# Strassen's seven products for K, three Q blocks and two feature groups, placed ahead of attention, in a fused attention and feed-forward kernel

## Chip, cores and metric

One Trainium2 chip; the kernel uses one NeuronCore. The metric is the device time of one execution in microseconds (us). The time before the change is the median of three runs.

## What is computed

A gated sum of two branches over one sequence of 2048 tokens with 640 features. Branch `a` is attention with 32 heads of 20 features in four segments of 512 tokens, with a running memory (M, z) that each segment reads and then adds to. Branch `b` is a gated feed-forward layer with 1728 hidden features. Cut to what matters:

```python
x = A_x                                            # (1, 2048, 640)
q, k, v = x @ wq, x @ wk, x @ wv                   # 32 heads of 20
for s in range(4):                                 # segments of 512 tokens
    logits = qs @ ks.T * 20**-0.5 + mask           # causal, inside the segment
    a_dot = softmax(logits) @ vs
    a_mem = (phi(qs) @ M) / (phi(qs) @ z + 1e-6)   # phi(t) = t+1 if t>0 else exp(t)
    o = g * a_mem + (1 - g) * a_dot                # g = sigmoid(beta), per head
    M, z = M + phi(ks).T @ vs, z + phi(ks).sum(0)
a = concat(o) @ wo
b = (silu(x @ w1) * (x @ w3)) @ w2                 # w1, w3: 640 x 1728
gate = sigmoid((x * gate_w).sum(-1))
out = gate * a + (1 - gate) * b
```

## The kernel before

The work is transposed: features lie on the 128 partitions, the 512 tokens of a segment (called a chunk `c`) along the free axis. 640 features make five blocks of 128 (`KB = 5`, index `kb` for the contraction, `mb` for blocks of Q or K outputs). The 1728 hidden features make 13 blocks of 128 and one of 64, in five groups of up to three: `GROUPS = [[0,1,2],[3,4,5],[6,7,8],[9,10,11],[13,12]]`.

Every dense product is made in three passes. A float32 operand is split in a high half (a rounded copy) and a low half (the rest), each an `FR` (float32r) tile, and high·high, high·low and low·high are added up in one PSUM bank: `PASSES = ((0,0),(0,1),(1,0))`. A projection of one output block for one chunk (`proj`, L267) is thus 5 x 3 = 15 matmuls of 128x512. The high half of a weight tile is a CAST and the low half a subtraction, both on POOL (L185 and L190; 640 columns each); the high half of an activation is cast by ACT, the low half subtracted by DVE or POOL (`split`, L116 and L117). PSUM is used as eight banks that are handed out in turn (`bank_tile`).

Weight tiles `W` live in a ring of six (`NW = 6`): a new one is written when the tile six before it has been used last. Raw weights come in by DMA, mostly on SP's queue, two at a time (`NRAW = 2`). `w_get` asks for a weight, and `w_step`, called after each few matmuls, loads and splits ahead.

The program has a head, a middle and a tail. The head (the list `head`) runs Q blocks 0 and 1, V, K and one more Q block of chunks 0 and 1 (`A`), with the writes of the memory (`memory_turn`: four transposes of phi(K); `memory_write`: four small matmuls). In the middle, attention for the 128 heads in four-head steps ("quads", 40 slots each) is laid between dense work: lists of jobs (`seg`) are spread over the attention's slots in proportion to their cost (`credit`). The first such stretch of dense work before is Q blocks 3 and 4 of chunks 0 and 1, groups 0 and 1 of the feed-forward layer and the up projections of group 2; the second begins with group 2's down projection and group 3. PE's order is the order of the program text; the other engines' orders are set by a scheduler from priorities and dependencies.

For a head, `s_fill` makes scores that DVE reduces to row maxima (L654), `t_fill` makes transposed scores that ACT exponentiates (L688) and POOL masks (L693), and `pv_quad` multiplies with V. The tiles `qk` (two buffers) hold the Q and K rows of two head pairs each, loaded by POOL's DMA queue (`load_pair`, L624).

`ffn_up` does for each chunk a gate product, ACT's tanh (L533), DVE's product (L534), an up product, DVE's product (L542) and the split in `ht` (ACT L116, POOL L117). `ffn_down` adds the products with w2 into `acc` (first group: ACT copies, L599; later ones: DVE adds, L601). `parts` (L290) makes from a Q or K block the high and low half and phi.

Of the kernel before, what the change touches and what calls it, by code (L numbers as in the profile page):

```python
# [38 lines left out]
def gated_mix(ctx: ExitStack, tc: tile.TileContext, xT, w01, wqk, wv, w13, w2, w2h, wo, beta, out):  # L39
# [28 lines left out]
    def constants():  # L68
        make_identity(nc, ident)
        nc.gpsimd.memset(mask, 0.0)  # L70
        nc.gpsimd.affine_select(mask[:, 384:], mask[:, 384:], pattern=[[-1, P]], base=0,
                                channel_multiplier=1, compare_op=ALU.is_ge, fill=BIG)
        for v in vg:
            nc.gpsimd.memset(v[:, :, VG:], 0.0)
        one = cp.tile([P, KB, L], F32, tag="oall", name="one", bufs=1)[:, 0]
        nc.gpsimd.memset(one, -1.0)
        for i in range(4):
            nc.gpsimd.tensor_copy(qk[i // 2][:, 1, i % 2], one)
# [42 lines left out]
    def bank_tile(name, hold=None):  # L121


        k = free.pop(0)
# [8 lines left out]
    def filled():  # L133

        free.extend(held)
        held.clear()
# [20 lines left out]
    items, tiles = [], {}  # L157

    def w_add(src, n, queue=nc.sync):
        items.append((src, n, queue))  # L160
        return len(items) - 1

    early, raws, clock = [], [], dict(step=0, oldest=2, next=2)

    def w_load():
        k = clock["next"]
        src, n, queue = items[k]
        if k in EARLY:
            if k % 2 == 0:
                early[:] = [sp.tile([P, 2, 1280], F32, tag="P32", name=f"wr{k}", bufs=NP)]  # L170
            raw = early[0][:, k % 2]
        else:
            raw = sp.tile([P, D + 2], F32, tag="wraw", name=f"wr{k}", bufs=NRAW)
        queue.dma_start(raw[:, :n], src)
        raws.append([k, raw, n, clock["step"]])
        clock["next"] += 1

    def w_split():
        k, raw, n, _ = raws.pop(0)
        w = sp.tile([P, 2, D + 2], FR, tag="W", name=f"W{k}", bufs=NW)  # L180
        tiles[k] = w
        if k < 7:
            split(w[:, :, :n], raw[:, :n], lo=nc.vector.tensor_sub)
        else:
            hi = nc.gpsimd.tensor_copy(w[:, 0, :n], raw[:, :n])  # L185
# [4 lines left out]
            last["low"] = nc.gpsimd.tensor_sub(w[:, 1, :n], raw[:, :n], w[:, 0, :n].bitcast(F32))  # L190

    def w_step():
# [3 lines left out]
        if raws and raws[0][0] in EARLY:  # L196
            if clock["step"] >= 6 + 2 * raws[0][0]:
                w_split()
        elif raws and raws[0][0] < clock["oldest"] + NW and \
                clock["step"] - raws[0][3] >= (AGE if "exp" in last or raws[0][0] < 7 else 2 * AGE + 1):  # L200
            w_split()
        if sum(r[0] not in EARLY for r in raws) < NRAW and clock["next"] < min(len(items), clock["oldest"] + NW + NRAW):
            w_load()

    def w_get(i, oldest=None):

        while i not in tiles:
            if not raws or raws[-1][0] < i and len(raws) < NRAW:
                w_load()
            else:  # L210
                w_split()
        clock["oldest"] = i if oldest is None else oldest
        return tiles[i]

# [225 lines left out]

    def memory_turn(c, mb):
# [76 lines left out]
    hts = {}  # L518

# [59 lines left out]
    def ffn_down(cs, js, idx, last=()):  # L579
        first = js[0] == 0  # L580
        w2s = [w_get(i, idx[0]) for i in idx]
        for c in cs:
            if first:
                accs[c] = slot(f"acc{c}")[:, :KB * L].rearrange("p (b n) -> p b n", b=KB)
            for fb in range(KB):
# [132 lines left out]
    def o_sums(c):  # L718
# [4 lines left out]
        after(22 if c < NSEG - 1 else 3, o_scale, c, er)  # L723
# [86 lines left out]
    def attention():  # L810

        for m in range(-1, NQUAD + 2):
            for n in range(40):
# [14 lines left out]
                elif n in ((24, 36) if m < 0 else (BIG + (1 if m > 1 else 7), SMALL + 1)) and m + 1 < NQUAD:  # L828
# [43 lines left out]
    def job_up(cs, j):  # L872
        return (4 if j < NF else 2) * 3.5, ffn_up(cs, j, plan_up([j])[0])
# [49 lines left out]
    head = qa + job_v(A)  # L923
    load_wide(1)
    ka, turns, writes = jobs_k(A)
    q2 = job_q(A, 2)
    head += ka + q2[:1] + turns + q2[1:] + writes
# [42 lines left out]
    for n, (_, g) in enumerate(head):  # L970
# [3 lines left out]
        if n == 0:  # L974
            constants()
        elif n == 2:
            selection()
        elif n == 7:
            gates()
    stores(True)  # L980
    att = attention()
# [115 lines left out]
```

## Time and profile before

| what | value |
|---|---|
| time, median of 3 runs (lowest to highest) | 1099.46 us (1099.38 to 1099.56) |
| profiled execution, first to last instruction | 1098.7 us |
| PE matmul busy | 1093.1 us (99%), 6289 records |
| DVE, POOL, ACT busy | 603.1, 584.2, 381.9 us |
| first Q blocks begin, V begins | 4.5 us, 20.2 us |
| first attention matmul (tile `s`) | 124.8 us |
| last attention score matmul (tile `s`) | 980.2 us |
| granted TensorE clock | full |

The profiled span and the median time differ by 0.8 us, which lies around the span. Busy time of PE counts the stretches covered by a matmul's record; records overlap, so a group's mean duration (some 400 ns for 128x512) isn't the spacing of its matmuls, which is read from two starts in the timeline. A line number in a row of the profile is that of the kernel before; tile names there have their numbers left out.

### The profile page before, as it was taken

The page shows a single profiled execution, that of the slowest core. Times are in us where ns is not written, and L with a number is a line of the kernel's source. Part 1 is how long each engine was busy: PE and PEld are TensorE (multiplying, and loading weights), DVE is VectorE, ACT ScalarE, POOL GpSimd, SP SyncE. Part 2 cuts the span into 40 slices and gives each one's busy share as a digit, 9 for nine tenths or more (in the row PEclk, how much of TensorE's full clock was granted, in tenths as well). Part 3 has the DMA queues.
Part 4 walks back from the last instruction along what each step waited for, and adds up shares of the span by engine and source line. Part 5 has one row for each costly group of instructions (what it writes and reads, how often), then busy time and mean ns, then how long its engine had stood idle before and what let it go on. Part 6 is the DMA issues. An engine that isn't in the chain of part 4 may idle for free.

```text
span 1098.7 us, 17910 instructions
## 1 busy us (share of the span) xinstructions
PE 1093.1 (99%) x6289; PEld 853.6 (78%) x6289; DVE 603.1 (55%) x1716; ACT 381.9 (35%) x829; POOL 584.2 (53%) x729
## 2 busy tenths in 40 slices
PE   9999999999999999999999999999999999999998
PEld 7988887777777777778977777777777777777787
DVE  6032474356555554566153678975657765551575
ACT  6244233443233122145244543424333332223020
POOL 5055556366366363566066447656674655565263
PEclk9999999999999999999999999999999999999999
DMA  9266943334355234435367966445664343432122
GB/s 314 105 207 222 284 123 82 95 83 117 77 141 124 58 85 124 137 83 184 112 201 264 298 216 185 112 148 140 161 149 111 96 113 97 111 102 89 52 79 96
DMA packets 87978, 153.21 MB, mean 139 GB/s; under 512 B 11632, under 2 KB 25872, under 8 KB 87888
## 3 DMA queue, kind: packets, MB, share of 16 engines
q1 hardware_dynamic: 63472, 106.30, 30.3%
q0 software_dynamic: 20384, 38.68, 15.6%
q10 hardware_dynamic: 4032, 7.08, 1.8%
q8 instruction: 50, 0.82, 0.3%
q14 instruction: 40, 0.33, 0.1%
HBM read 96.56 MB, written 54.54 MB: 138 GB/s over the span
## 4 chain that ended last, share of the span: by engine, by line
PE 99%; DMA 0%; ACT 0%; DVE 0%; SPq 0%; issue 0%
PE g L267 18%; PE f L593 18%; PE u L267 17%; PE o L703 7%; PE v L398 7%; PE op L852 6%; PE k L267 6%; PE q L267 5%; PE s L647 5%; PE t L682 4%; PE nd L365 2%; PE pm L462 1%; PE q L338 1%; PE gt L783 1%; PE pkt L447 1%; PE rr L777 0%
## 5 line engine op out<-in xcount | busy, mean ns | idle before, releaser
L654 DVE CUSTOM_DVE_ANT_0 junk<-s,mask 128x256 bf16<-128x256 f32 (+3 forms) x512 | 250.4, 489 | 106.1 <-PE s L647 74.0
L688 ACT ACTIVATE P<-t 128x512 f32<-128x512 f32 (+1 forms) x384 | 172.5, 536 | 187.7 <-PE t L682 145.1
L267 PE MATMUL g<-X,W 128*128 128x512 f32 x840 | 208.9, 398 | 0.1
L190 POOL TENSOR_TENSOR W<-wr,W 128x640 fp32r<-128x640 f32 (+1 forms) x126 | 198.8, 1583 | 2.5
L267 PE MATMUL u<-X,W 128*128 128x512 f32 x780 | 196.9, 399 | 0.0
L593 PE MATMUL f<-ht,W 128*128 128x512 f32 (+1 forms) x825 | 196.4, 395 | 0.0
L185 POOL CAST W<-wr 128x640 fp32r<-128x640 f32 (+1 forms) x126 | 92.6, 739 | 195.1 <-PE v L398 44.6
L693 POOL TENSOR_SCALAR_AFFINE_SELECT P<-P 128x256 f32<-128x256 f32 x192 | 93.6, 497 | 179.5 <-ACT P L688 179.2
L267 PEld LDWEIGHTS g<-X,W 128*128 128x128 f32 x840 | 155.8, 188 | 37.3 <-DVE m L654 0.4
L593 PEld LDWEIGHTS f<-ht,W 128*128 128x128 f32 x825 | 153.1, 188 | 36.3
L267 PEld LDWEIGHTS u<-X,W 128*128 128x128 f32 x780 | 144.0, 188 | 34.5 <-ACT P L688 0.3
L117 POOL TENSOR_TENSOR ht<-ft,ht 128x512 fp32r<-128x512 f32 x52 | 67.5, 1298 | 91.1 <-ACT ht L116 91.0
L624 POOL DMA_DIRECT2D qk<-qkd x128 | 83.3, 652 | 0.5 <-issue 0.2
L647 PE MATMUL s<-qk 60*128 60x256 f32 (+3 forms) x512 | 77.7, 346 | 0.0
L267 PE MATMUL k<-X,W 128*128 128x512 f32 x300 | 77.2, 404 | 0.0
L703 PE MATMUL o<-P,vg 128*32 128x512 f32 (+3 forms) x1024 | 75.5, 435 | 0.1
L533 ACT ACTIVATE ft<-g 128x512 f32<-128x512 f32 x52 | 31.2, 600 | 126.5 <-PE g L267 113.8
L534 DVE SCALAR_TENSOR_TENSOR fu<-ft,g 128x512 f32<-128x512 f32 x52 | 35.6, 685 | 67.9 <-ACT ft L533 58.8
L398 PE MATMUL v<-W,X 128*128 128x320 f32 (+1 forms) x480 | 72.1, 311 | 0.2 <-ACT P L688 0.2
L398 PEld LDWEIGHTS v<-W,X 128*128 128x128 f32 x480 | 71.2, 189 | 0.9 <-ACT P L688 0.4
L116 ACT CAST ht<-ft 128x512 fp32r<-128x512 f32 x52 | 32.2, 619 | 109.9 <-DVE ft L542 108.1
L601 DVE TENSOR_TENSOR acc<-f,acc 128x512 f32<-128x512 f32 x65 | 44.8, 689 | 39.5 <-PE f L593 39.2
(125 smaller groups left out, 1209.3 us busy)
## 6 DMA issues: line engine op xcount, KB each, us to landing
qk<-qkd POOLq DMA_DIRECT2D x128, 240.0 KB, 4.1
wr<-in_w_dram SPq DMA_DIRECT2D x80, 320.0 KB
qkd<-qs SPq DMA_DIRECT2D x20, 512.0 KB
qkd<-ks SPq DMA_DIRECT2D x20, 512.0 KB
od<-oq SPq DMA_DIRECT2D x32, 256.0 KB
wr<-in_wo_dram SPq DMA_DIRECT2D x20, 320.0 KB
vg<-vd SPq DMA_DIRECT2D x16, 336.0 KB
xr<-in_xT_dram SPq DMA_DIRECT2D x20, 256.0 KB
```

What stands on the lines that cost most here:

```text
L117: (lo or nc.gpsimd.tensor_sub)(dst[:, 1], src, dst[:, 0].bitcast(F32))
L185: hi = nc.gpsimd.tensor_copy(w[:, 0, :n], raw[:, :n])
L190: last["low"] = nc.gpsimd.tensor_sub(w[:, 1, :n], raw[:, :n], w[:, 0, :n].bitcast(F32))
L267: nc.tensor.matmul(ps, w[:, a, kb * P:(kb + 1) * P], x[:, b, kb, :], start=n == 0, stop=n == 14)
L398: nc.tensor.matmul(ps[:, :n1 - n0], x[:, a, kb, lb * P:(lb + 1) * P], wvt[kb][:, b, n0:n1], start=n == 0, stop=n == 14)
L593: nc.tensor.matmul(ps[:, :n1 - n0], w, h, start=n == 0, stop=n == len(ms) - 1)
L624: here(nc.gpsimd.dma_start(t[64 * i:64 * i + RH], qkd[c][RH * (h + i):RH * (h + i + 1)]))
L647: nc.tensor.matmul(ps[i][:, o:o + w], q[:, qb * P:(qb + 1) * P], key[:, :w], start=n == 0, stop=n == len(todo) - 1, skip_group_check=True)
L654: r = nc.vector.tensor_tensor_reduce(out=junk[:, :w], in0=ps[i][:, o:o + w], in1=mask[:, L - w:], scale=1.0, scalar=-3.0e38, op0=ALU.add, ...
L688: last["exp"] = nc.scalar.activation(pairs[2 * m + k]["P"][:, i, o:o + n], ps[i][:, b:b + n], AF.Exp, scale=SCALE)
L693: nc.gpsimd.affine_select(d, d, pattern=[[0, 2], [0, n], [1, P]], base=0, channel_multiplier=-1, compare_op=ALU.is_ge, fill=0.0)
L703: nc.tensor.matmul(ps[32 * i:32 * i + 32, kb * P:], heads[2 * p + i]["v"][:, kb], pairs[p + i // 2]["P"][:, i % 2, o:o + n], start=kb == 0 ...
```

## The change

Two output blocks of weights (columns of the weight matrices: two blocks of K or Q, or the gate and the up block of one feature block) times two chunks make a two-by-two product. Over the first four contraction blocks (two and two) it is now made with seven block products in place of eight (the form with shared sums); the fifth contraction block is added the ordinary way. One such "unit" has 54 matmuls in place of 60. There are ten: K0 with K1, K2 with K3, K4 with Q2, Q3 with Q4, and feature blocks 0 to 5. All run for chunks 0 and 1, in the head, before the first attention matmul; the down projection of group 0 too. What stood in the first two dense stretches of the middle moves up accordingly, and those stretches are shorter.

- `build_sums` loads eight blocks of x again and builds four sums of activations (T1 to T4, two blocks each, high and low half) while V runs. T1 and T2 lie in the two `qk` buffers, T3 and T4 in two of the three buffers of attention's P.
- `w_add_unit` makes four weight tiles per unit: the first block as it is (`all`, 640 columns), two sums (`sum0`, 640; `sum1`, 512) and the fifth contraction part of the second (`low`, 384). The sums are five DVE operations (four of 256 columns, one of 128), L211 to L215 of the new kernel; casts and subtractions of the tiles stay on POOL (now L220 and L225).
- Three more raw buffers (`wrs`, in the third P buffer).
- `unit` runs the products in four banks: `a`, `w`, `x`, `y`. Bank `a` is copied out by ACT into the SBUF tile W after its first six matmuls and then added to further; DVE adds `w` to W, `y` to V (an SBUF copy of `x`), W to V, `x` to W (tile `g`), and `y` to W.
- `take` hands the four results on: one is read from PSUM, three from SBUF tiles. In K's units they go to `parts`; in the feed-forward units the subtraction for `ht` is DVE's, POOL's before.
- The down projections of groups 0 and 1 run chunk 1 first, with two banks side by side (`lead`).
- The fills of `qk`'s row of -1 move from POOL to two DVE memsets in the last unit (`fixed_rows`), followed by the loads of the first two head pairs.
- `o_scale` of chunk 0 comes 14 slots after the sums in place of 22.

On PE, K's blocks before were runs of 15 matmuls with transposes and memory writes between (names: tile<-stationary and moving operand; `pkt` transposes, `pm` memory writes). Rows of the kernel before:

```order
L267 MATMUL k_1_695<-X_103,W_594 128x512 x12
L462 MATMUL pm_0_711<-V_302,pkn_0_693 128x147 x4
L267 MATMUL k_1_695<-X_103,W_594 128x512 x3
L447 MATMUL pkt_0_743<-ident,pk_0_680 128x128 x4
L267 MATMUL k_1_750<-X_105,W_594 128x512 x12
```

Now the unit of K2 and K3 stands there (bank `a` is called k_k2k; T1 and T2 are qk_90 and qk_91):

```order
L542 MATMUL k_k2k_807<-X_103,W_668 128x512 x6
L542 MATMUL w_k2k_815<-qk_91,W_675 128x512 x3
L666 MATMUL pkt_0_821<-ident,unit 128x128 x4
L542 MATMUL w_k2k_815<-qk_91,W_675 128x512 x3
L542 MATMUL x_k2k_832<-qk_90,W_731 128x512 x3
L666 MATMUL pkt_0_836<-ident,unit 128x128 x4
L542 MATMUL x_k2k_832<-qk_90,W_731 128x512 x3
L542 MATMUL x_k2k_832<-X_105,W_743 128x512 x3
L666 MATMUL pkt_1_850<-ident,vg_92 128x128 x4
L542 MATMUL k_k2k_807<-X_103,W_668 128x512 x6
L666 MATMUL pkt_1_863<-ident,vg_93 128x128 x4
L542 MATMUL k_k2k_807<-X_103,W_668 128x512 x3
```

Bank `a` is taken up again after 21 matmuls of the unit and three groups of transposes.

On DVE the end of a K block was two operations, each of which reads its product from PSUM:

```order
L299 TENSOR_TENSOR ks_0_681<-k_0_647,ks_0_681 128x512
L301 SCALAR_TENSOR_TENSOR pk_0_680<-k_0_647,phi_t 128x512
L299 TENSOR_TENSOR ks_1_731<-k_1_695,ks_1_731 128x512
L301 SCALAR_TENSOR_TENSOR pk_1_730<-k_1_695,phi_t 128x512
L299 TENSOR_TENSOR ks_1_780<-k_1_750,ks_1_780 128x512
L301 SCALAR_TENSOR_TENSOR pk_1_779<-k_1_750,phi_t 128x512
```

Now, from the last product of the unit of K0 and K1 to the first addition of the next unit (tile `unit` holds W, V and `g`; `ws` and `wr` are weight sums and raw weights):

```order
L595 TENSOR_TENSOR unit<-unit,y_k0k_734 128x512
L348 TENSOR_TENSOR ks_1_766<-unit,ks_1_766 128x512
L350 SCALAR_TENSOR_TENSOR unit<-unit,phi_t 128x512
L348 TENSOR_TENSOR ks_1_786<-unit,ks_1_786 128x512
L211 TENSOR_TENSOR ws_798<-wr_635 128x256
L212 TENSOR_TENSOR ws_798<-wrs,wr_635 128x256
L350 SCALAR_TENSOR_TENSOR vg_92<-unit,phi_t 128x512
L350 SCALAR_TENSOR_TENSOR vg_93<-unit,phi_t 128x512
L558 TENSOR_TENSOR unit<-unit,w_k2k_815 128x512
```

Seven of the nine have no operand in PSUM, and the last but one reads W before ACT may copy the next `a` into it.

On DVE a feed-forward product was two operations with a PSUM operand, between attention's reductions:

```order
L143 TENSOR_TENSOR ns_101<-m_1843,nh_2169 128x16
L667 STREAM_TRANSPOSE mr<-ns_101 32x32 x4
L534 SCALAR_TENSOR_TENSOR fu_3_2245<-ft_3_2244,g_3_2217 128x512
L542 SCALAR_TENSOR_TENSOR ft_3_2244<-fu_3_2245,u_3_2253 128x512
L654 ISA junk,m_2098<-s_0_0_2272,mask 128x512
```

Now, in the unit of feature block 4 (`f_ff` is its bank `a`):

```order
L639 SCALAR_TENSOR_TENSOR fu_3_1814<-fu_3_1814,unit 128x512
L116 TENSOR_TENSOR ht_3_1762<-fu_3_1844,ht_3_1762 128x512
L558 TENSOR_TENSOR unit<-unit,w_ff_1887 128x512
L116 TENSOR_TENSOR ht_3_1761<-fu_3_1814,ht_3_1761 128x512
L213 TENSOR_TENSOR wr_1593<-ws_1867,wr_1593 128x256
L215 TENSOR_TENSOR wr_1593<-wr_1593,wrs 128x128
L214 TENSOR_TENSOR wr_1593<-wr_1593 128x256
L637 SCALAR_TENSOR_TENSOR fu_4_1915<-fu_4_1915,f_ff_1879 128x512
L577 TENSOR_TENSOR unit<-unit,y_ff_1921 128x512
L578 TENSOR_TENSOR unit<-unit 128x512
L587 TENSOR_TENSOR unit<-unit,x_ff_1895 128x512
```

The low halves of `ht` and the weight sums of the next unit stand ahead of L577, which empties the bank `y` that PE takes up again 9 matmuls later.

The diff, cut to its core:

```diff
@@ weights: prods beside items
+    def w_add_unit(src0, src1, queue=nc.sync):
+        items.extend((src, D, queue) for src in (src0, src1))
+        r = len(items) - 2
+        prods.extend((("all", (r,)), ("sum0", (r, r + 1)), ("sum1", (r + 1,)), ("low", (r + 1,))))
+        return list(range(len(prods) - 4, len(prods)))
@@ def w_split():
+        elif kind == "sum0":
+            low = raws[rs[1]][0]
+            sums[rs[1]] = t = f_tile(f"ws{k}")
+            a11, a12, a15 = raw[:, :2 * P], raw[:, 2 * P:4 * P], raw[:, 4 * P:D]
+            a21, a22, a25 = low[:, :2 * P], low[:, 2 * P:4 * P], low[:, 4 * P:D]
+            nc.vector.tensor_add(t[:, 2 * P:], a21, a22)
+            nc.vector.tensor_sub(t[:, :2 * P], a11, a21)
+            nc.vector.tensor_sub(a11, t[:, 2 * P:], a11)
+            nc.vector.tensor_sub(a12, a12, a11)
+            nc.vector.tensor_sub(a15, a15, a25)
...
+            hi = nc.gpsimd.tensor_copy(w[:, 0, :n], src)
...
+            last["low"] = nc.gpsimd.tensor_sub(w[:, 1, :n], src, w[:, 0, :n].bitcast(F32))
@@ def build_sums(cs):   (for i in 0, 1)
+            nc.vector.tensor_sub(b22, b22, b12)
+            nc.vector.tensor_sub(b12, b12, b11)
+            nc.vector.tensor_add(b11, b22, b11)
+            split(out(2, i), b11, lo=nc.vector.tensor_sub)
...
@@ def unit(cs, name, idx, take, W, V, G):
+        yield from product(a, U, 0, B(c0, 0), 2, True, True)
+        nc.scalar.copy(W, a)
+        S0 = w_get(wa, w0)
+        yield from product(w, S0, 0, T(2), 2, True, True)
+        nc.vector.tensor_add(W, W, w)
+        S1 = w_get(wb, w0)
+        yield from product(x, S1, 2 * P, T(1), 2, True)
+        A2 = w_get(wl, w0)
+        yield from product(x, A2, 2 * P, B(c1, 4), 1, False, True)
+        nc.scalar.copy(V, x)
+        yield from product(a, U, 2 * P, B(c0, 2), 2)
+        yield from product(a, U, 4 * P, B(c0, 4), 1, False, True)
+        take(0, c0, a)
+        yield from product(y, S1, 0, T(3), 2, True, True)
+        nc.vector.tensor_add(V, V, y)
+        nc.vector.tensor_add(V, V, W)
+        yield from product(x, S0, 2 * P, B(c1, 2), 2)
+        yield from product(x, S0, 4 * P, B(c1, 4), 1, False, True)
+        nc.vector.tensor_add(g, W, x)
+        take(0, c1, g)
+        take(1, c1, V)
+        yield from product(y, A2, 0, T(4), 2)
+        yield from product(y, A2, 2 * P, B(c0, 4), 1, False, True)
+        nc.vector.tensor_add(W, W, y)
+        take(1, c0, W)
...
@@ def ffn_unit: take
+                nc.scalar.activation(u, ps, AF.Tanh, scale=0.5)
+                nc.vector.scalar_tensor_tensor(u, u, 1.0, ps, op0=ALU.add, op1=ALU.mult)
...
+                nc.vector.scalar_tensor_tensor(us[c], us[c], 0.5, ps, op0=ALU.mult, op1=ALU.mult)
+                split(hts[c, j], us[c], lo=nc.vector.tensor_sub)
+            if i == 0 and c == cs[0] and j == GROUPS[1][-1]:
+                fixed_rows()
+                for p in range(2):
+                    load_pair(p)
+        yield from unit(cs, f"ff{j}", idx, take, *(rest[3:5] + rest[6:] if j % 2 else rest[:3]))
@@ head and middle
-    head = qa + job_v(A)
+    head = qa + [braid(chain(job_v(A)), (0, build_sums(A)), 3)]
...
+    head += jobs_qk(A, ((K0, K1), (K2, K3), (K4, (0, 2)), ((0, 3), (0, 4))))
+    head += [job_unit(A, j) for j in GROUPS[0]] + [job_down(A, 0)] + [job_unit(A, j) for j in GROUPS[1]]
-    seg = job_q2(A, 3)
-    g = jobs_group(A, 0)
-    seg += [braid(chain(g[:2]), job_read(1), 3, at=(7, 10, 13, 16, 18, 22, 25, 28))] + g[2:] + jobs_group(A, 1) + jobs_up(A, 2)
+    seg = [job_down(A, 1)]
+    g = jobs_group(A, 2)
+    seg += [braid(chain(g[:2]), job_read(1), 3, at=(7, 10, 13, 16, 18, 22, 25, 28))] + g[2:] + jobs_up(A, 3)
-    d = job_down(A, 2)
-    u = [job_up(A, j) for j in GROUPS[3][:2]]
+    d = job_down(A, 3)
-    seg = [d, braid(chain(u), o1, 5), o2] + [job_up(A, j) for j in GROUPS[3][2:]] + [(0, load_shares(A[:1])), job_down(A, 3)]
+    seg = [braid(d, o1, 3, at=(13, 15, 17, 19, 20)), (0, load_shares(A[:1])), o2]
```

More of the change, by code (lines that the diff above doesn't have):

```diff
@@ L72, in constants, with fixed_rows @@
                                 channel_multiplier=1, compare_op=ALU.is_ge, fill=BIG)
[L73 to L78, printed above, removed]
+    def fixed_rows():
+        for t in qk:
+            nc.vector.memset(t[:, 1].bitcast(F32), -1.0)
+        nc.vector.memset(vg[0][:, :, VG:], 0.0)
     def gates():
```

216 lines of the change are left out of this document (185 added, 31 removed).

## The prediction, made before the changed kernel ran

> **What bounds the kernel now.** I read the page's spans and chain of waits first, then PE's waits, then the timeline for the spacing of matmuls, then DVE and POOL.
>
> ```profile
> span 1098.7 us, 17910 instructions
> PE 1093.1 (99%) x6289; PEld 853.6 (78%) x6289; DVE 603.1 (55%) x1716; ACT 381.9 (35%) x829; POOL 584.2 (53%) x729
> ...
> PE 99%; DMA 0%; ACT 0%; DVE 0%; SPq 0%; issue 0%
> ...
> PE warm L921 <- DVE zero L918: 1.3, 1, 1.3
> PE v L398 <- ACT P L688: 0.2, 1, 0.2
> ```
>
> The chain that ended last is PE for 99%, and PE's longest wait is the one at the start. So time follows the count of PE's matmuls as long as no other engine makes PE wait; the others are half idle on average. What a dense 128x512 matmul is worth stands in undisturbed runs of the timeline (columns: start, length, engine, line, operation, tiles, count):
>
> ```profile
> 112.68 12.17 PE L267 MATMUL q<-X,W 128*128 128x512 f32 x51
> 124.78 1.27 PE L647 MATMUL s<-qk 60*128 60x512 f32 x8
> 471.97 7.13 PE L267 MATMUL g<-X,W 128*128 128x512 f32 x30
> 478.94 1.55 PE L267 MATMUL u<-X,W 128*128 128x512 f32 x6
> 63.28 0.60 PE L447 MATMUL pkt<-ident,pk 128*128 128x128 f32 x4
> 66.53 1.16 PE L462 MATMUL pm<-V,pkn 128*128 128x147 f32 x8
> ```
>
> From one start to the next: 12.10 us / 51 = 0.237, and 6.97 us / 30 = 0.232 us each. The last two rows price what stands between K's products: 0.60 us for four transposes, 1.16 us for eight memory matmuls.
>
> **What it saves.** The program has 3275 full float32r matmuls of 128x512 in place of 3335: ten units, six fewer in each. All other matmuls keep their count. 60 x 0.232 to 0.237 is 13.9 to 14.2 us; I take 14.0. Attention is cut in as many visits as before, so I credit nothing for fewer changes between kinds. This is the ceiling of the gain: 1098.7 - 14.0 = 1084.7 us of span.
>
> **What it adds.** Durations of one operation:
>
> ```profile
> 7.41 0.42 DVE L117 TENSOR_TENSOR w01s<-wr,w01s 128x256 fp32r<-128x256 f32 x1
> L601 DVE TENSOR_TENSOR acc<-f,acc 128x512 f32<-128x512 f32 x65 | 44.8, 689 | 39.5 <-PE f L593 39.2
> L185 POOL CAST W<-wr 128x640 fp32r<-128x640 f32 x121 | 88.5, 735 | 191.5 <-PE v L398 44.6 <-PE f L593 40.7 <-PE u L267 19.6
> L190 POOL TENSOR_TENSOR W<-wr,W 128x640 fp32r<-128x640 f32 x121 | 191.0, 1583 | 2.4
> L599 ACT COPY acc<-f 128x512 f32<-128x512 f32 x20 | 11.8, 588 | 24.0 <-PE f L593 19.9 <-DMA qk<-mr 2.3 <-issue 1.7
> L468 POOL TENSOR_SCALAR_AFFINE_SELECT mt<-mt 128x147 f32<-128x147 f32 x12 | 4.5, 373 | 12.6 <-ACT mt L466 12.6
> 0.94 0.27 DVE L918 MEMSET zero<- 128x256 uint32 x1 [0.94 <-PEq L1084]
> 0.00:57.00 57.00, 55.42 (x312) 48.61 (x313) 18.71 (x28) 23.83 (x53) 19.59 (x33) 1.00 0.57 202
> ```
>
> A feed-forward unit lasts 54 x 0.232 = 12.5 us on PE. POOL casts and subtracts 640 + 640 + 512 + 384 = 2176 columns, 2176/640 x (0.735 + 1.583) = 7.9 us, 63% of it. DVE has eleven operations of 512 columns (0.69 each, five with a PSUM operand, six between SBUF tiles) and five weight sums (four of 0.42, one about 0.3, an estimate by its width): 9.6 us, 77%. ACT has two copies, two tanh and two casts, under 4 us. A unit of K with the memory work of the unit before has 16 transposes and 16 memory matmuls too, 12.5 + 2.4 + 2.3 = 17.2 us; DVE 4.1 us with PSUM operands, 4.8 between tiles, 2.0 of sums, 10.9 in all; POOL 7.9 plus four times some 1.15 us (two selects and a copy or addition), 12.5 us or 73%.
>
> By busy time nothing here exceeds PE. But DVE and POOL get in each other's way, and only on operations that read two SBUF tiles:
>
> ```profile
> 450.60 4.05 POOL L190 TENSOR_TENSOR W<-wr,W 128x640 fp32r<-128x640 f32 x2
> 451.88 1.34 DVE L557 TENSOR_TENSOR acc<-acc,sh 128x512 f32<-128x512 f32 x1
> 453.15 0.68 DVE L601 TENSOR_TENSOR acc<-f,acc 128x512 f32<-128x512 f32 x1
> 453.86 1.34 DVE L557 TENSOR_TENSOR acc<-acc,sh 128x512 f32<-128x512 f32 x1
> 455.84 0.69 DVE L557 TENSOR_TENSOR acc<-acc,sh 128x512 f32<-128x512 f32 x1
> L786 DVE TENSOR_TENSOR oall<-on,gm 128x512 fp32r<-128x512 f32 x15 | 13.6, 915 | 2.1 <-ACT gm L785 2.1
> L557 DVE TENSOR_TENSOR acc<-acc,sh 128x512 f32<-128x512 f32 x12 | 11.7, 971 | 1.6 <-DMA sh<-ed 1.3
> ```
>
> L557 reads two SBUF tiles: 0.69 us when POOL is idle, 1.34 us beside POOL's subtractions; those, too, last 4.05 us for two where 3.17 would do. L601 with its PSUM operand stays at 0.68 us in the midst of it. Over all their executions L786 and L557 lost 0.22 and 0.28 us each (means 0.915 and 0.971 less 0.69), beside a POOL that is busy 53%. I take 0.25 and scale by POOL's share: 0.30 us in a feed-forward unit, 0.34 in a K unit (estimates). Before, K's and the layer's DVE operations read PSUM and lost nothing; now 11 of 16 in a feed-forward unit are exposed.
>
> Feed-forward units: 9.6 + 11 x 0.30 = 12.9 us of DVE against 12.5 on PE. DVE falls back by 0.4 us per unit, and bank `y`, which PE takes up again 9 matmuls (2.1 us) after it ended, waits for DVE's queue; six units cost 2.2 us. Bounds: nothing if the waits are as short as the smallest (9.6 us leaves 2.9 us of room), 4.0 us each if every operation of POOL went first.
>
> K units: between two of them, DVE's queue has the nine operations shown in the order up to the last reader of W, then ACT copies the next `a` into W, and only then may PE go on in bank `a`. Without waits: one operation from PSUM and five between tiles at 0.69, two sums at 0.42, ACT's copy 0.59, and some 0.17 us by which a matmul's result comes after its successor's start (an estimate, record 0.40 less spacing 0.23): 5.7 us. PE arrives after 21 x 0.232 + 3 x 0.60 = 6.7 us. With seven waits of 0.34 it is 8.1 us: PE waits 1.4 us, at two hand-overs (into K2/K3 and into K4/Q2) 2.8 us. After K4/Q2, W holds a Q block of chunk 0, which has no phi; that chain is 1.4 us shorter and costs nothing. Bounds: 0 and 3 us each.
>
> The rest: `build_sums` has 16 operations on DVE (11 us) and 8 casts on ACT (5 us) in the V stretch, where DVE is busy 18.7 of 57 us: hidden, and the room is over 25 us even if its eight loads come late. The two memsets of 1024 columns, 4 x 0.27 = 1.1 us each, stand in the last unit, which has no sums for a successor (2.0 us less); behind them on POOL's queue wait the loads of the first pairs and the third weight tile of the next down projection. I give 0.5 us, bounds 0 and 2. The shorter `o_scale` delay leaves 51 matmuls, 12 us, between the sums and their use: nothing. PE asks for the weight tiles 1 to 2 us after POOL can have written them (an estimate from the order and the durations above): nothing, unless POOL waits as DVE does.
>
> Sum: 1098.7 - 14.0 + 2.8 + 2.2 + 0.5 = 1090.2 us of span; the median lies 0.8 us above this span, so 1091.0 us.
>
> [...]
>
> **Rivals.** (1) All of it is hidden: waits stay under the room, 1099.5 - 14.0 = 1085.5. For it: DVE's slack of 2.9 us per unit and banks enough for two units. Against: the K hand-over has 1.0 us of room for seven exposed operations.
>
> (2) The two engines exclude each other fully. Exposed DVE operations and POOL's add up to 6.1 + 7.9 = 14.0 us in a feed-forward unit against 12.5, and 6.8 + 12.5 = 19.3 against 17.2 in two K units: 6 x 1.5 + 2 x 2.1 = 13.2 us lost, 1098.7, no change. Against it: at 451.88 to 453.86 a pair takes 1.98 us where the two alone take 1.58 + 0.69 = 2.27, so starts overlap; with that ratio, 0.87, the 14.0 become 12.2.
>
> (3) The other side: DVE loses its turn to queued work of POOL and becomes the bound. That this occurs is shown here:
>
> ```profile
> 12.38 4.48 DVE L117 TENSOR_TENSOR X<-xr,X 128x512 fp32r<-128x512 f32 x2 [0.68 <-ACT X L116]
> 13.75 2.56 POOL L117 TENSOR_TENSOR X<-xr,X 128x512 fp32r<-128x512 f32 x2
> ```
>
> Two operations of DVE took 4.48 us while POOL made its own, two of them in a row. If DVE waited for all of POOL, a feed-forward unit would take 9.6 + 0.87 x 7.9 = 16.5 us and a K unit 10.9 + 0.87 x 12.5 = 21.8: 6 x 4.0 + 2 x 4.6 = 33 us, 1118.7. The gain is gone from a mean wait of 0.42 us per exposed operation; the rows show 0.22 to 0.28.
>
> (4) Attention, with less dense work beside it, makes PE wait. Its first stretch has 540 dense matmuls for 9.5 quads, about 20.7 us per quad, with some 14.8 us of DVE work (estimates), 72%. Against it:
>
> ```profile
> 600.00:700.00 100.00, 99.99 (x637) 75.97 (x632) 74.24 (x220) 46.48 (x100) 54.26 (x71) 1.00 0.72 216
> ```
>
> In this stage (columns: PE, weight loads, DVE, ACT, POOL) DVE was busy 74% and PE didn't wait. At 0.5 us per quad over some 15 quads it would add 7.5 us: about 1098.
>
> **Chances.** The forecast with its own range 1088 to 1097: 0.49. Rival (1), 1084.5 to 1088: 0.24. Rival (2): 0.12. Rival (3): 0.09, most of it beyond 1101.7. Rival (4): 0.06, half of it within 0.2%. A difference of 0.2% (2.2 us) is about what the measurement can tell from none. Faster: 0.49 + 0.24 + 0.03 and some of (2), 0.79; same 0.12; slower 0.09. The range 1084.5 to 1099.5 leaves out (3) and the upper part of (2).
>
> **What will show it.** Right: 60 fewer records of PE, PE's waits in the K units on ACT's copy into W or on DVE's phi, some 1.4 us each, and on DVE at bank `y` in feed-forward units; DVE's tile-to-tile operations at about 1 us there; no waits in attention. Wrong: PE waiting for the W tiles of POOL (the rings are then too short); PE's waits near `s` or `t` (rival 4); DVE busy over 95% from the first to the last unit (rival 3); or PE's spacing in the units far from 0.232 us.

## The result, and the profile after

The changed kernel takes 1115.1 us (median of four runs, 1113.4 to 1118.4) against 1099.4 before: ratio 1.0145, 95% interval 1.0129 to 1.0162. It is slower by 15.7 us, where 8.5 us less were forecast. All times below are of undisturbed executions; one of the five of the kernel with several edits, 1312.35 us at a mean clock of 0.753, is left out. The profiled execution of the changed kernel is the longest of its four; from its page:

```profile
span 1116.7 us, 17989 instructions
...
PE 1091.5 (98%) x6229; PEld 846.8 (76%) x6229; DVE 704.4 (63%) x1848; ACT 397.6 (36%) x857; POOL 614.6 (55%) x751
```

The 60 matmuls are gone (6229 records for 6289), and they gave what they should: in the timeline a feed-forward unit lasts from 139.75 to 152.31 us, 12.56 us or 54 x 0.2326.

```profile
139.75 1.55 PE L542 MATMUL f_ff<-X,W 128*128 128x512 f32 x6
152.31 1.55 PE L542 MATMUL f_ff<-X,W 128*128 128x512 f32 x6
```

So 32.0 us were lost in this execution against the ceiling of 1084.7 us of span, some 3 us more than in the median one. (Time and span of one execution differ by about 1.7 us throughout, here 1118.4 - 1116.7; the 0.8 us of the forecast seem to compare two executions.) Where they were lost, a table by stage shows: busy time of PE (first pair of columns behind the length) and, third from the end, the granted clock, for the head, attention's first dense stretch, the second, and two stages behind them. First the kernel before, then the changed one:

```profile
0.00:125.00 125.00, 123.42 (x663) 105.58 (x664) 39.09 (x60) 53.31 (x116) 57.41 (x90) 1.00 0.65 218
125.00:378.00 253.00, 252.89 (x1446) 193.39 (x1446) 139.70 (x468) 81.34 (x179) 135.08 (x167) 1.00 0.42 111
378.00:627.00 249.00, 248.73 (x1422) 199.71 (x1420) 127.36 (x336) 95.18 (x207) 130.63 (x161) 1.00 0.52 161
627.00:762.00 135.00, 134.99 (x878) 102.82 (x878) 102.39 (x325) 54.46 (x120) 77.88 (x99) 1.00 0.60 171
762.00:1098.00 336.00, 333.08 (x1894) 252.08 (x1886) 194.53 (x530) 97.61 (x211) 183.24 (x213) 1.00 0.39 104
```

```profile
0.00:237.00 237.00, 229.03 (x1104) 188.89 (x1106) 154.70 (x223) 91.79 (x181) 141.75 (x158) 0.99 0.47 156
237.00:441.00 204.00, 197.36 (x1192) 146.37 (x1194) 135.53 (x460) 67.66 (x155) 104.99 (x141) 0.98 0.47 118
441.00:646.00 205.00, 199.79 (x1192) 159.87 (x1184) 117.03 (x315) 87.81 (x196) 106.68 (x141) 0.98 0.59 182
646.00:780.00 134.00, 133.01 (x864) 101.22 (x861) 101.45 (x323) 52.82 (x117) 77.61 (x99) 1.00 0.58 164
780.00:1116.00 336.00, 332.29 (x1891) 250.48 (x1887) 195.68 (x530) 97.48 (x211) 183.59 (x213) 1.00 0.39 104
```

PE's idle time grew by 6.4 us in the head (8.0 less 1.6), 6.5 in the first stretch, 4.9 in the second, 1.8 behind them. A slower clock, shown below, costs another 8.5 us. That makes 28.1 of the 32.0. By the spacing of matmul starts beyond what their columns take, the growth is 8.5, 12.9, 8.5 and 2.1 us, clock and short stalls included (with the median spacing of each shape before as the price it is 9.7, 11.5, 8.2 and 2.5, so the split is good to some 1.4 us); the terms below are in the first measure. PE's waits, largest first:

```profile
PE pkt L666 <- DVE pk L350: 2.6, 1, 2.6
PE t L915 <- DMA qk<-mr: 2.6, 1, 2.6
PE nd L414 <- DVE m L887: 2.1, 2, 1.6
PE pkt L666 <- DVE vg L350: 1.9, 1, 1.9
PE f L808 <- ACT ht L115: 1.5, 2, 1.2
...
PE o L936 <- DVE pq L350: 1.2, 1, 1.2
PE f L808 <- DVE ht L116: 1.1, 1, 1.1
PE s L880 <- DVE oq L940: 1.0, 1, 1.0
...
PE f_ff L542 <- ACT unit L552: 0.7, 1, 0.7
...
PE k_k2k L542 <- ACT unit L552: 0.6, 1, 0.6
```

Five of them are paid twice (they start at 75, 282, 389, 480 and 568 us). One microsecond behind the first, and windows around or behind all five, show the clock, third from the end:

```profile
80.00:81.00 1.00, 1.00 (x7) 0.80 (x5) 0.00 (x0) 0.00 (x0) 0.84 (x2) 0.50 0.00 0
77.20:84.00 6.80, 6.24 (x26) 5.06 (x27) 2.32 (x6) 3.95 (x8) 3.49 (x4) 0.75 0.13 38
280.00:290.00 10.00, 8.43 (x43) 6.88 (x43) 6.97 (x30) 3.23 (x10) 5.28 (x10) 0.83 0.65 175
389.00:400.00 11.00, 8.42 (x62) 4.88 (x62) 4.82 (x14) 4.86 (x11) 4.86 (x8) 0.84 0.23 74
480.00:486.00 6.00, 5.06 (x16) 3.98 (x17) 3.93 (x14) 1.21 (x5) 4.70 (x7) 0.72 0.64 211
570.00:576.00 6.00, 5.35 (x20) 4.44 (x21) 1.19 (x2) 1.01 (x2) 0.00 (x0) 0.72 0.64 238
```

6.8 x 0.25, 10 x 0.17, 11 x 0.16, 6 x 0.28 and again 6 x 0.28 are 1.7 us each: after a wait the clock was 0.50 for 3.41 us (79.43 to 82.84 us the first time), five times, 8.5 us in all. The mean clock of 0.992 over the span agrees (8.9 us by its three digits).

### The profile page after: what moved, and what is told of

Same layout as the page of the kernel before. It is cut to its first block, busy times and chain, and to the rows that moved or that the text cites. A ratio compares the mean times of both kernels' runs of the same rounds, so it can differ in the third digit from the quotient of the medians.

```text
span 1116.7 us, 17989 instructions
## 1 busy us (share of the span) xinstructions
PE 1091.5 (98%) x6229; PEld 846.8 (76%) x6229; DVE 704.4 (63%) x1848; ACT 397.6 (36%) x857; POOL 614.6 (55%) x751
## 4 chain that ended last, share of the span: by engine, by line
PE 90%; DVE 7%; issue 1%; ACT 1%; DMA 1%; ACTq 0%; SPq 0%; DVEq 0%
PE f L826 14%; PE g L316 13%; PE u L316 12%; PE o L936 7%; PE op L1085 6%; PE v L447 6%; PE s L880 5%; PE t L915 4%; PE q L316 3%; PE k L316 3%; PE f L808 2%; PE x_ff L542 2%; PE f_ff L542 2%; PE nd L414 2%; DVE junk L887 2%; PE y_ff L542 1%
## 5 line engine op out<-in xcount | busy, mean ns | idle before, releaser
L225 POOL TENSOR_TENSOR W<-wr,W 128x640 fp32r<-128x640 f32 (+2 forms) x117 | 186.6, 1599 | 1.7
L220 POOL CAST W<-wr 128x640 fp32r<-128x640 f32 (+2 forms) x117 | 87.5, 752 | 153.8 <-PE f L826 38.2
L316 PE MATMUL g<-X,W 128*128 128x512 f32 x660 | 166.0, 400 | 0.1
L826 PE MATMUL f<-ht,W 128*128 128x512 f32 (+1 forms) x681 | 164.5, 396 | 0.6 <-DVE m L887 0.6
L316 PE MATMUL u<-X,W 128*128 128x512 f32 x600 | 153.5, 402 | 0.0
L316 PEld LDWEIGHTS g<-X,W 128*128 128x128 f32 x660 | 122.7, 189 | 29.4 <-DVE m L887 0.5
L316 PEld LDWEIGHTS u<-X,W 128*128 128x128 f32 x600 | 111.4, 190 | 26.9 <-issue 0.4
L880 PEld LDWEIGHTS s<-qk 60*128 60x128 f32 x512 | 46.7, 185 | 26.4 <-issue 17.0
L915 PE MATMUL t<-qk 62*128 62x256 f32 (+3 forms) x512 | 62.7, 321 | 3.5 <-DMA qk<-mr 2.6
L915 PEld LDWEIGHTS t<-qk 62*128 62x128 f32 x512 | 46.7, 186 | 16.6 <-issue 6.5
```

Source lines behind the costliest of these rows:

```text
L220: hi = nc.gpsimd.tensor_copy(w[:, 0, :n], src)
L225: last["low"] = nc.gpsimd.tensor_sub(w[:, 1, :n], src, w[:, 0, :n].bitcast(F32))
L316: nc.tensor.matmul(ps, w[:, a, kb * P:(kb + 1) * P], x[:, b, kb, :], start=n == 0, stop=n == 14)
L826: nc.tensor.matmul(ps[:, :n1 - n0], w, h, start=n == 0, stop=n == len(ms) - 1)
L880: nc.tensor.matmul(ps[i][:, o:o + w], q[:, qb * P:(qb + 1) * P], key[:, :w], start=n == 0, stop=n == len(todo) - 1, skip_group_check=True)
L915: nc.tensor.matmul(ps[i][:, o:o + L - kb * P], key[:, kb * P:(kb + 1) * P], q[:, kb * P:], start=n == 0, stop=n == len(todo) - 1, skip_gro ...
```

## The experiments

**Placement alone.** The kernel before, with the same work moved ahead of attention as ordinary products:

```diff
     head += ka + q2[:1] + turns + q2[1:] + writes
+    head += job_q2(A, 3) + jobs_group(A, 0) + jobs_up(A, 1)
```

(and the two stretches and the 14 slots of `o_scale` as in the change).

> The kernel before with the same work moved ahead of attention as in the change (Q3 and Q4, groups 0 and 1 of the feed-forward layer), all as ordinary products: no unit, no weight sum, 3335 full matmuls as before. By the theory that attention with less dense work beside it makes PE wait: what the changed kernel loses from its first attention matmul on comes back, 12.9 us in the first stretch and 8.5 us in the second (excess of PE's spacing, 16.3 less 3.4 and 12.3 less 3.8), some 2 us behind it, so 1099.4 + 21 to 25 = 1120 to 1125 us. By the theory that the units cost what is missing (their DVE and POOL work, their hand-overs, what they leave behind): 1099 to 1102 us.

1122.6 us, ratio 1.0215 (1.0197 to 1.0232), +22.9 us against its own runs of before. Its stretches lose what the changed kernel's do; its head does not:

```profile
0.00:240.00 240.00, 238.37 (x1162) 199.58 (x1162) 60.28 (x91) 75.67 (x153) 112.03 (x138) 1.00 0.43 144
240.00:446.00 206.00, 198.61 (x1193) 147.76 (x1196) 134.83 (x460) 67.50 (x155) 103.62 (x138) 0.98 0.47 118
446.00:650.00 204.00, 197.90 (x1188) 158.70 (x1190) 118.44 (x314) 87.52 (x195) 106.12 (x141) 0.99 0.58 183
```

Its trace has the longest waits of the changed kernel's stretches too: 1.56 us for the memory read (`nd`), 1.83 us for `mr`, 2.58 us for phi. Some 1.9 us before its first scores, for the loads of the first pairs, are its own.

So the change is two things: the placement costs 23 us with no unit in it, and the units in the same place give 1122.6 - 1115.1 = 7.5 us of their 14.0.

**Fewer units.** Only K's and Q's, with groups 0 and 1 back in the middle:

```diff
-    head += [job_unit(A, j) for j in GROUPS[0]] + [job_down(A, 0)] + [job_unit(A, j) for j in GROUPS[1]]
...
```

> Only the four units of K and Q; groups 0 and 1 are ordinary products in the middle again, as before. 24 matmuls fewer, 24 x 0.235 = 5.6 us. By the theory of thin attention: Q3 and Q4 alone are missing from the first stretch (174 in place of 188 units of cost for 38 heads), so attention loses 0 to 2 us; the head keeps the wait of the changed kernel between its first two units (2.5 us and some 2.2 us of slower matmuls behind it): 1099.4 - 5.6 + 4.7 + 0 to 2 = 1098.5 to 1100.5 us. By the theory that each unit costs some 3 us more than it saves: 1099.4 - 5.6 + 4 x 3.2 = 1106.6 us.

1112.7 us, ratio 1.0122 (1.0108 to 1.0136): off by 13 us, through my edit. Here the memsets and loads of the first pairs came after the last unit, and the first scores waited for them, 6.18 us and then 2.84 us:

```profile
144.72 0.79 PE L880 MATMUL s<-qk 60*128 60x512 f32 x1 [6.18 <-DMA qk<-qkd]
```

With `fixed_rows()` and `load_pair` issued from inside the last unit:

> Only the four units of K and Q, as in the run of that kind before, but the two memsets and the loads of the first head pairs are issued from inside the last unit (as in the changed kernel), so that the first scores don't wait for them (6.4 us and 3.4 us there, with 1.2 us of slower score matmuls). By the theory of thin attention the rest holds: 1099.4 - 5.6 + 4.7 to 5.5 for the wait between the first two K units and the slower matmuls behind it, and up to 1 in the first quad: 1098.5 to 1101.5 us. If units as such cost more, by work that they leave to DVE and POOL in attention: 1104 us or more.

1101.8 us, ratio 1.0017 (1.0009 to 1.0026), 0.3 us above the range. With attention nearly as dense as before (174 units of cost in its first stretch for 188) PE waits there for 0.9 and 0.6 us alone; the hand-over between the first two units (1.84 and 0.56 us) is left.

Then group 0's units too, group 1 as ordinary products in the first stretch:

```diff
-    seg = [job_down(A, 1)]
+    seg = jobs_group(A, 1)
...
```

> The changed kernel with feature blocks 3 to 5 as ordinary products at the start of the first stretch; units for K, Q and feature blocks 0 to 2. 42 matmuls fewer, 9.8 us. By the theory of thin attention: the first stretch has 174 units of cost for 38 heads (131.6 in the changed kernel, 188 before), so its loss falls from 12.9 to some 0 to 3 us; the second stretch is that of the changed kernel and keeps its 8.5 us if it is thinness there as well, the head keeps some 7: 1105 to 1108 us. By the theory that the units cost 3.2 us each: 1099.4 - 9.8 + 7 x 3.2 = 1112 us, with the loss in the head or right behind it.

1110.7 us, ratio 1.0096 (1.0082 to 1.0110). As expected the first stretch's growth is small (2.1 us by spacing, 5.5 less 3.4) and the second keeps 6.7, the head 5.8; these are of its fastest execution (1108.2 us), and the median is 2.7 us above the range.

**The memory read of chunk 1**, later in the same thin stretch:

```diff
-    seg += [braid(chain(g[:2]), job_read(1), 3, at=(...))] + g[2:] + jobs_up(A, 3)
+    u = jobs_up(A, 3)
+    seg += g + [braid(chain(u[:2]), job_read(1), 3, at=(...))] + u[2:]
```

> The changed kernel with the memory read of chunk 1 beside group 3's up projections in place of group 2's: the reads leave attention's first quads, in which DVE also has the additions of group 1's down projection. By the theory that thin quads as such make PE wait: the wait of the read on DVE's row maxima at 282 us goes from there and others of its kind come, 1113 to 1117 us. By the theory that it is the pile of DVE work in the first quads: 4 to 6 us less, 1109 to 1111 us.

1109.0 us, ratio 1.0091 (1.0075 to 1.0106): 6.1 us less than the changed kernel. The waits at 282 and 389 us are both gone, though no job was taken out of the stretch. By the timeline its first eight quads last 16.7 to 19.9 us from one first `t` to the next, those before 23 to 25 us; from 264 us to the end of the stretch no wait over 0.3 us is left. The two slow stretches behind those waits are gone with them (the clock is 1.00 from 272 to 433 us), 3.4 us in this execution.

**The hand-over between K's units:**

```diff
-        nc.vector.tensor_add(W, W, y)
-        take(1, c0, W)
+        Z = W if name[0] == "f" else f_tile(f"uz{name}")
+        nc.vector.tensor_add(Z, W, y)
+        take(1, c0, Z)
...
-            if n >= 3 and n % 2 and steps:
+            if n in (5, 8, 11, 13, 14, 15, 16, 17) and steps:
```

> The changed kernel with the hand-over between units of K and Q opened: the last result goes to a tile of its own in place of W, so that ACT may copy the next unit's bank `a` into W at once, and the transposes of the unit before come two to four products later. By the theory that DVE's operations held up by POOL's subtractions make phi(K) and W late there: the waits of 1.9 and 0.6 us, the slower matmuls behind them (2.2 us) and 0.9 us at the first feed-forward unit go, 1115.1 less 4.5 to 5.5 = 1109.6 to 1110.6 us. By the rival that DVE is simply behind there whatever stands in between: PE waits at the next transposes, 1113 us or more.

1111.4 us, ratio 1.0108 (1.0095 to 1.0122): 3.8 us less, 0.8 us above the range. In its timeline neither the transposes nor bank `a` wait, and there is no slow stretch behind them; a wait of 0.40 us for a weight tile of POOL has come ahead of them:

```profile
76.23 1.62 PE L542 MATMUL k_k2k<-X,W 128*128 128x512 f32 x6
...
78.39 0.60 PE L667 MATMUL pkt<-ident,vg 128*128 128x128 f32 x4
```

**One operation of four columns.** In the changed kernel's second stretch:

```profile
561.14 1.38 POOL L220 CAST W<-wr 128x640 fp32r<-128x640 f32 x2
561.93 3.68 DVE L462 TENSOR_SCALAR gate<-gate 128x4 f32<-128x4 f32 x1
562.49 3.09 POOL L225 TENSOR_TENSOR W<-wr,W 128x640 fp32r<-128x640 f32 x2
566.79 1.08 ACTq L903 DMA_DIRECT2D qk<-mr  x2
570.65 0.88 PE L666 MATMUL pkt<-ident,pk 128*128 128x128 f32 x4 [2.61 <-DVE pk L350]
```

This operation runs four times: twice it takes 0.17 us, once 1.44 us, and here it ends with POOL's second subtraction (565.61 and 565.58 us); the run with the later memory read shows 3.68 us at the same place (552.10 us), and with placement alone the four take 5.5 us in all, as here. It reads one SBUF tile, so the prediction's "only on operations that read two SBUF tiles" was too narrow, and the kernel before shows that already (0.17 us in its shortest execution):

```profile
552.27 1.49 DVE L413 TENSOR_SCALAR gate<-gate 128x4 f32<-128x4 f32 x1
```

In the changed kernel DVE's copy of the row maxima stands behind it, ACT's queue behind that copy's DMA, K's casts and phi behind ACT, and PE at the end.

```diff
-        nc.vector.tensor_scalar(e, e, TOP, None, op0=ALU.min)
-        nc.vector.tensor_scalar(g, e, 1.0, None, op0=ALU.add)
+        eng = nc.vector if c < 2 else nc.gpsimd
+        eng.tensor_scalar(g, e, TOP, 1.0, op0=ALU.min, op1=ALU.add)
+        eng.tensor_scalar(e, e, TOP, None, op0=ALU.min)
```

> The changed kernel with two operations of 128x4 elements (minimum and addition for chunk 2's and 3's gate) on POOL in place of DVE. In the changed kernel the second of them lasted 3.68 us on DVE at 561.9 us (0.17 elsewhere), while POOL made its subtractions; DVE's row maxima, the copy of them that ACT's queue starts, and K's phi stood behind it, and PE waited 2.6 us for that phi and ran some 1.9 us slower behind. By the theory that POOL's subtractions held that one operation: 1115.1 - 4.5 = 1110.6 us. By the theory that DVE has too much to do in thin quads: the wait stays, 1113 us or more.

1113.2 us, ratio 1.0124 (1.0108 to 1.0139), 1.9 us less. In time that is the second expectation (1113 us or more), and too near to the changed kernel's own scatter (1113.4 to 1118.4) to settle by it; but that one also said that the wait stays, and in the trace it doesn't. The chain is as told: DVE's queue goes on, phi is there before the transposes, and 0.75 us at the gate's own transpose remain of the 2.61.

```profile
565.52 0.27 PE L469 MATMUL ge<-ident,gate 128*8 128x128 f32 x1 [0.75 <-DVE gate L464]
567.02 0.60 PE L667 MATMUL pkt<-ident,pk 128*128 128x128 f32 x4
```

**Several together.** The changed kernel with these three edits and three banks side by side in the first down projections:

> The changed kernel with four edits: memory read later (6.1 us by the run above), the two of this call (4.5 to 5.5 and 4.5 us), and three banks in place of two side by side in the first two down projections, whose waits on the last ht are 1.4 and 1.7 us. If the losses are separate places, they add up: 1115.1 - 6.1 - 5 - 4.5 - 2 = 1097.5 us, just below the kernel before. If a wait that is taken away comes back at the next place: 1102 to 1107 us.

Four runs of 1102.1 to 1105.6 us, ratio 1.0039 (1.0025 to 1.0052): 11 us better than the changed kernel, near the sum of the single effects as measured (6.1 + 3.8 + 1.9 = 11.8, the banks not tried alone), and not the 17.6 that I expected; the time lies in the other expectation's range. Its fastest execution has no slow stretch (mean clock 1.000) and still loses 1100.3 - 1084.7 = 15.6 us, with no wait over 1.3 us. The same with group 1 as ordinary products and the read where it was:

> Units for K, Q and feature blocks 0 to 2, blocks 3 to 5 as ordinary products in the first stretch, with the hand-over, the gate on POOL and three banks in the first down projection. 1110.7 us without the three edits; hand-over and the wait at the first feed-forward unit 4.5 to 5, gate 2 to 4, banks 1.5: 1100.5 to 1102.5 us if the places add up. By the theory that the second stretch is too thin whatever is mended: 1104 us or more.

1101.2 us, ratio 1.0024 (1.0013 to 1.0035), as expected. That the places are separate and add up fits this, but was not tried edit by edit: the 9.4 us gained here are more than the single effects in the changed kernel.

**Q3 and Q4 in the middle,** group 1's down projection at the end of the head:

> The mended kernel with Q3 and Q4 as ordinary products at the start of the first stretch (12 matmuls more, 2.8 us) and the down projection of group 1 ahead of attention, so that the first quads stand beside Q blocks as before and not beside DVE's additions into acc; the stretch is thinner by 7 units of cost (145.6 in place of 152.5 with the down projection, 188 before). By the theory that what stands on DVE beside the quads decides, and not how thin they are: the 4 us of excess in the first quads go, 1103.5 + 2.8 - 4 = 1102 to 1103 us, with no wait before the second stretch. By the theory of thinness: 1106 us or more, with new waits in the first stretch.

1111.5 us, ratio 1.0113 (1.0100 to 1.0127): my first expectation was wrong, and the number is in the range of the other (1106 or more), partly through the edit itself. The moved down projection asks at once for the `ht` of the units just made (2.77 and 1.63 us; the mean clock of 0.995 is worth another 5.5 us over the whole span), and the first quad's `t`, 39 dense matmuls behind its last scores, waits for the row maxima that ACT's DMA brings (`mr`):

```profile
212.70 0.70 PE L820 MATMUL f<-ht,W 128*128 128x512 f32 x2 [2.77 <-ACT ht L115]
260.84 1.21 PE L927 MATMUL t<-qk 62*128 62x512 f32 x8 [3.45 <-DMA qk<-mr]
```

**The units that pay:** K's and Q's alone, loads from inside the last unit, hand-over opened.

> Only the four units of K and Q (24 matmuls fewer, 5.6 us), with the hand-over between them opened as in the run of that name; the feed-forward layer in the middle as before. By the theory that the losses are separate places: the run with these units alone took 1101.8 us, of which 4.0 to 4.5 us are the hand-over between the first two units: 1097.3 to 1097.8 us, below the kernel before by 0.2%. If something else takes that place: 1100 us or more.

1096.9 us, ratio 0.9975 (0.9966 to 0.9985): 0.4 us under the range, and faster than both kernels: than the one before by 2.6 us of the 5.6 that 24 matmuls are worth. Its page has 6265 records of PE, 24 fewer.

**Thin quads.** That kernel with a first stretch as thin as the changed kernel's, and with the memory read away from the first quads:

```diff
-    seg = [braid(chain(g[:2]), job_read(1), 3, at=(...))] + g[2:] + jobs_group(A, 1) + jobs_up(A, 2)
+    seg = jobs_group(A, 0)
+    g = jobs_group(A, 1)
+    seg += [braid(chain(g[:2]), job_read(1), 3, at=(...))] + g[2:]
...
-    seg = [d, braid(chain(u), o1, 5), o2] + ...
+    seg = v + [d, braid(chain(u), o1, 5), o2] + ...    # v = jobs_up(A, 2)
```

> The last but two kernel (units of K and Q alone, hand-over opened, 1096.9 us) with a first stretch as thin as in the changed kernel: the up projections of group 2 go from its end to the start of the second stretch (131.4 in place of 173.6 units of cost for 38 heads, 131.6 in the changed kernel), which becomes thicker than before. The memory read stands beside group 1's up projections, away from the first quads. By the theory that thin quads as such make PE wait: the first stretch loses what it loses in the changed kernel, 8 to 13 us more than now, 1105 to 1110 us. By the theory that single places do it, where DVE's own work (memory read, additions, an operation held by POOL) falls between a quad's row maxima and the next visit: quads of 16 to 20 us without excess, and 1097 to 1100 us.

1100.4 us, ratio 1.0008 (0.9999 to 1.0017): 3.5 us more than without, not 8 to 13, and a little above the other theory's range. All of it is lost up to the first quads, where PE waits 1.3 us for the loads of a head pair and one slow stretch follows (a clock of 0.97 over 60 us, 1.8 us); behind them quads of 17 to 21 us follow for 150 us, memory read included, and PE is not idle at all:

```profile
130.00:190.00 60.00, 57.78 (x329) 42.63 (x329) 35.25 (x127) 21.67 (x48) 39.49 (x48) 0.97 0.48 111
190.00:340.00 150.00, 150.00 (x916) 114.23 (x913) 95.66 (x322) 54.04 (x121) 82.52 (x108) 1.00 0.46 121
```

**What thinness does.** A quad's last scores (`s`) lead to its first `t` through DVE's row maxima, a transpose and ACT's DMA (`mr`). Before, that visit came after 57 dense matmuls; in the changed kernel after 39. First two rows before, then four of the changed kernel:

```profile
277.84 0.45 PE L647 MATMUL s<-qk 60*128 60x384 f32 x4
291.95 0.64 PE L682 MATMUL t<-qk 62*128 62x512 f32 x6
```

```profile
379.37 0.45 PE L880 MATMUL s<-qk 60*128 60x384 f32 x4
385.67 0.84 DVE L900 STREAM_TRANSPOSE mr<-ns 32x32 f32<-32x32 f32 x4
389.03 0.50 PE L880 MATMUL s<-qk 60*128 60x512 f32 x2
392.10 0.73 PE L915 MATMUL t<-qk 62*128 62x512 f32 x6 [2.57 <-DMA qk<-mr]
```

Over the first eight quads the way from the start of such a group of `s` to `t` is 13.4 to 15.6 us before; in the changed kernel it is 13.9 to 15.4 in the first three and 9.3 to 12.8 in the next five; in the thin kernel 9.3 to 12.7 behind the first quad, with no wait of `t` over 0.3 us. So 9.3 us do when nothing comes in between. At 386.5 us, where ACT's queue issues `mr`, something did: `t` could start only 5.6 us after the transposes' end, where the thin kernel's 2.9 us (183.7 to 186.6) were enough at one visit. The DMA engines' mean share (second column from the end) in these two intervals was 0.54 and 0.19:

```profile
386.50:392.10 5.60, 3.03 (x15) 1.96 (x13) 2.61 (x7) 1.22 (x2) 1.99 (x2) 1.00 0.54 133
```

```profile
183.70:186.60 2.90, 2.90 (x14) 2.15 (x14) 0.00 (x0) 0.76 (x2) 1.50 (x1) 1.00 0.19 34
```

That other transfers made `mr` late is argued from these rows; no run took them away.

## Why the prediction was wrong, step by step

- *The saving, 14.0 us.* Right: 60 fewer records, feed-forward units at 0.2326 us per matmul.
- *K's hand-overs, 2.8 us, two of 1.4.* One of two came. Into the unit of K2 and K3 PE waited 1.85 us for phi and 0.56 us for bank `a`, then ran at half speed at a cost of 1.7; into K4 and Q2 it did not wait. Opening it gave 3.8 us. The price of 1.4 us had a wrong reading in it: 0.60 us is the length of a record of four transposes, not their spacing, which in the kernel before is 0.35 us (63.28 to 63.63 us). PE then arrives after 5.9 us and not 6.7, and the same sum gives 2.2 us of wait, near the 2.4 that came; that the total of 2.8 lies near the measured 3.8 is luck, since the second wait did not come and the clock was not in it. I had taken 0.34 us for an operation beside POOL; the four rows below lost 1.1, 0.7, 1.35 and, in the two of `vg`, nothing:

```profile
71.43 1.79 DVE L350 SCALAR_TENSOR_TENSOR unit<-unit,phi_t 128x512 f32<-128x512 f32 x1
73.14 1.36 DVE L348 TENSOR_TENSOR ks<-unit,ks 128x512 fp32r<-128x512 f32 x1
74.42 1.77 DVE L211 TENSOR_TENSOR ws<-wr 128x256 f32<-128x256 f32 x1
76.45 1.28 DVE L350 SCALAR_TENSOR_TENSOR vg<-unit,phi_t 128x512 f32<-128x512 f32 x2
```

- *Feed-forward units, 2.2 us at bank `y`.* None. PE waited 0.7 us for ACT's copy of bank `a` on entering the first of them, and nowhere inside.
- *The rest, 0.5 us.* Low: the two down projections waited 2.6 us for the last `ht`, which the forecast left out.
- *Attention, nothing.* This is the step that failed. I forecast "no waits in attention" and gave rival (4) a chance of 0.06 and a price of 7.5 us. It cost 12.9 us in the first stretch and 8.5 in the second, 21.4 in all with four of the five slow stretches, and the run with placement alone shows such a loss without a unit (22.9 us). My argument was a window with DVE at 74% and no wait; in the changed kernel's first stretch DVE is busy 135.53 of 204 us, 66%. The share of an engine does not tell whether a chain through DVE, ACT, a DMA queue and PE ends in time. The number to read in the first stretch was the slack of that chain: the `s` to `t` interval of 13 to 16 us before, of which the change takes up to 5. Less cover alone was not enough: the thin kernel ran 150 us without idle time, and moving one job, the memory read, brought back 6.1 us. A long wait came where cover was short and DVE or a DMA had other work in the chain; the memory read, which was moved, is shown to be such a place, that of `mr` is argued. In the second stretch this slack is not the reason: the interval stays at 16 us or more there, and PE's longest waits are for DVE's phi of K (2.6 us), for `pq`, phi of Q (1.2 us), and for DVE's copy of a quad's product with V, `oq` (1.0 us), of which only the first was followed up.
- *Rivals (2) and (3).* In the units neither came: POOL and DVE held each other up (from 62 to 237 us L578, which adds two SBUF tiles, took 0.68 to 2.11 us, 1.50 at the median, and POOL's subtractions of 640 columns 1.87 and 1.69 us on average for 1.58 before), but PE was covered. Rival (3)'s 1118.7 us is the nearest number on record, by luck: DVE was busy 70% from 62 to 237 us, not over 95%. What rival (3) supposes, DVE held up by queued work of POOL, came at one place that the forecast left out, in attention: 3.68 us for 0.17, until the second of two subtractions in a row had ended.
- *The clock.* Not in the sum at all: 1.7 us behind each of five waits, 8.5 us, which the figures by stage contain.

Of the 32.0 us: head 8.5, first stretch 12.9, second stretch 8.5, the rest 2.1. Shown by experiments: the placement as a whole (22.9 without units), and in it 6.1 (place of the read); in the head 3.8 (hand-over); and in the trace, though not in time, the gate's chain. What causes the smaller waits of 0.3 to 1.2 us in the first quads and the second stretch was not tried one by one and stays open.

## What to carry over

Work that stands beside a latency-bound chain is its cover: before moving it, measure how long the chain has now from its last producer to its consumer, and how much of that the move takes, place by place; and what else of DVE and the DMA queues falls into it; an average busy share says nothing on it. Take the part of a change that leaves the cover alone (here four units of ten with the hand-over opened, which gave 2.6 us, where all ten cost 15.7). And price a wait of PE at its length plus what the clock can take behind it, here 1.7 us.

## What the hardware did that I had not expected

- Waits of PE of 1 to 2.6 us were followed by a granted clock of 0.50 for 3.41 us, 1.7 us lost, in five places of one execution; other waits of 1.2 us (at 168 and 618 us) were not. By the trace's clock records the five stretches begin at 79.4, 284.2, 393.5, 482.2 and 571.0 us, that is 60, 32, 26 and 26 times 3.41 us apart. Counted off in periods of 3.41 us from these starts, PE was idle 1.1 to 2.6 us of the one period ahead of each, and at most 0.9 us of any other whole period; the two waits of 1.2 us lie across a boundary. This is one execution; with placement alone four waits of 1.6 to 2.6 us stand beside a mean clock of 0.995, which is 5.6 us of 1119.6, the worth of three such stretches. Executions of one kernel differ by this: four of the mended kernel had spans of 1100.3, 1101.8, 1102.8 and 1103.9 us at mean clocks of 1.000, 0.998, 0.997 and 0.996.
- A DVE operation on 128x4 elements that reads one SBUF tile lasted 3.68 us beside POOL's weight work (casts and subtractions from 561.14 to 565.58 us), 22 times its shortest 0.17 us.
